# A chunk pair's triangular solve four pieces later in a slot pipeline, and DMA transfers in program order

## The chip, the core and the metric

The kernel runs on one core of one Trainium2 chip. The metric is the device time of one execution in microseconds. Engines are named as in the profile: PE (TensorE matrix multiplication), DVE (VectorE), ACT (ScalarE), POOL (GpSimd), SP (SyncE, whose queue issues every DMA transfer of this kernel). Tiles in PSUM are the banks that PE writes.

## What is computed

A linear recurrence with a decayed state over 768 steps (batch 4, 8 heads, head dimension 40), then a dense layer pair, then eight experts whose outputs are summed under weights that are normalised over tokens and experts.

```
for t in range(S):                                     # S = 768
    kt, vt, rt = (k[:, :, t], v[:, :, t], r[:, :, t])
    wt, at, bt = (w[:, :, t], a[:, :, t], b[:, :, t])
    y[:, :, t] = np.einsum('bhd,bhde->bhe', rt, state)
    Sa = np.einsum('bhde,bhe->bhd', state, at)
    state_decay = state * wt[:, :, None, :] - np.einsum('bhd,bhe->bhde', Sa, bt)
    state = state_decay + np.einsum('bhd,bhe->bhde', vt, kt)
...
h = x @ w_in                                           # 3072 x 320 by 320 x 2048
g = np.where(h > 0.0, h, alpha * (np.exp(np.minimum(h, 0.0)) - 1.0))
x = g @ w_out
...
for e in range(E):                                     # E = 8, 1024 wide
    h = np.maximum(x @ w1[e], 0.0)
    out += P[:, e:e + 1] * (h @ w2[e])
```

## The kernel before

The recurrence is cut into 24 chunks of 32 steps. Within a chunk the steps are made independent of each other by solving a unit lower triangular system of 32 x 32 for each of the 32 (batch, head) pairs. That solve is `tsolve_`: 31 columns, for each two DVE instructions, Tt = Wk x LT (L399) and Wk = Wk - Tt (L406). Wk starts as a copy of the identity, made by POOL (L394). LT, the matrix, is read from DRAM (L380), where E3 put it as Ad (four DMA transfers, L374) after PE (L355) and DVE (Am, L359) made it. The finished Wk goes to DRAM as Td in four transfers (L410) and comes back transposed as TT in four (L414). H2 (L447) multiplies by TT. Two chunks are solved together (`tsolve`), their instructions in turn.

The work of one chunk is a list of tokens, `PLAN["order"]`; one pass over it is a slot, and slot c finishes chunk c while it prepares chunks c+3 and c+4. E4 (L388) is the first matrix product of a slot. Then come, in this order: E3 for chunk c+3, H1, E2, H2, E1, H3, O1 (L500, transposes of VU into banks 2 and 3), H4, O2 (L355, whose result DVE masks as Gm, L359), O3a (L518, banks 2 and 3), O3b (L529). `prep` for chunk c+4 has its steps on DVE: wr and wq (L304, L305, from the loaded tile WA), the scan F (L308), the scan xE (L314). `xl` and `x` are the steps of the transposition of finished rows for the first dense layer, once in every two slots: two loads yt (L549), and for each half three transposes (L555, into bank 3), an ACT copy and X (L560, DVE, which reads bank 3). `ld`, `lu` and `lv` load WA and KE, VU, and rB and rO for coming chunks; yd (L537) stores the finished rows. `m` is half a unit of the first dense layer (L572 to L603), which fills PE between the steps of the recurrence; DVE makes g for it (L581).

There are 16 tokens `p` in a slot, counted here as p1 to p16. Each advances the pending solve by `PLAN["tp"]` = 3 steps. The token `T`, between p6 and p7 of an even slot c, puts the solve of chunks c+2 and c+3 in the queue; so it runs from p7 of the even slot to p11 of the odd one. The token `LT` is left out while a solve is pending.

From slot 2 on `pin_since` chains each instruction to the one before it on its engine, for the engines in `PINNED`: PE, DVE, ACT and POOL run in the order in which the code is written. SP isn't among them: a planner may put its transfers anywhere their data allow. Every transfer uses one of eight semaphores in turn, so that it waits for the landing of the transfer eight places ahead.

Behind slot 23 the rest of the first dense layer runs, and then the experts (`phase_b`), which take more than half of the time.

Of the kernel before, what the change touches and what calls it, by code (L numbers as in the profile page):

```python
# [22 lines left out]
PLAN = {  # L23
# [8 lines left out]
    "lead": 3,  # L32
}
# [64 lines left out]
def build(ctx, tc, r, k, v, w, a, b, w_in, w_out, wg, w1, w2, wa_d, kb_d, re_d, ro_d, vt_d, wp_d, consts, out, C, off):  # L98
# [11 lines left out]
    NB1 = NT // 256  # L110
    NTT = NT // 128
    V, A, G, T, SY = nc.vector, nc.scalar, nc.gpsimd, nc.tensor, nc.sync
    PINNED = {x.engine for x in (V, A, G, T)}
    pins = {}

    def traced():
        return nc.cur_bb.bb.instructions

    def pin_since(last):
        ins = traced()  # L120
        k = next(k for k in reversed(range(len(ins))) if ins[k] is last) + 1
        for x in ins[k:]:
            if x.engine in PINNED:
                if x.engine in pins:
                    tc.add_manual_dep(x, pins[x.engine], mybir.DependencyInfo(mybir.DependencyClass.NoSync, mybir.DependencyReason.DATA), reason="program order")
                pins[x.engine] = x.name
# [263 lines left out]
    def tsolve_(c):  # L390
        z = st[c]
        Wk = r2.tile([128, CI, C], F32, tag="Wk", name="Wk")
        tmp = r2.tile([128, CI * (C - 1)], F32, tag="Tt", name="Tt")
        G.tensor_copy(out=Wk.rearrange("p i t -> p (i t)"), in_=idk)  # L394
        for j in range(C - 1):
            ni = j // 4 + 1
            nt = C - 1 - j
            tv = tmp[:, 0:ni * nt].rearrange("p (i t) -> p i t", i=ni)
            V.tensor_tensor(  # L399
                out=tv,  # L400
                in0=Wk[:, 0:ni, j:j + 1].to_broadcast([128, ni, nt]),
                in1=z.LT[:, j, j + 1:C].unsqueeze(1).to_broadcast([128, ni, nt]),
                op=ALU.mult,
            )
            yield
            dve["T"] = V.tensor_tensor(out=Wk[:, 0:ni, j + 1:C], in0=Wk[:, 0:ni, j + 1:C], in1=tv, op=ALU.subtract)  # L406
            yield
        Td = drp.tile([B * H, C, C], F32, tag="Td", name="Td", bufs=3)
        for q in range(4):
            SY.dma_start(out=Td.rearrange("x (i q) t -> q x i t", q=4)[q], in_=Wk[q::4])  # L410
        z.TT = TTs[c % 4]
        for bb in range(B):
            bi = bb % 2
            SY.dma_start(out=z.TT[C * bb:C * bb + C, :, C * bi:C * bi + C], in_=Td[bb * H:(bb + 1) * H].rearrange("h s t -> s h t"))  # L414

    def tsolve(*cs):
        for _ in itertools.zip_longest(*(tsolve_(c) for c in cs)):
            yield
# [575 lines left out]
    with ExitStack():  # L994
# [13 lines left out]
        def try_xprep(new):  # L1008
            if new and not xgen:
                xp = ms["xp"]  # L1010
                if (late or xp == 0) and xp < NB1 and xp <= ms["n"] // NF1 + 1 and ("O3b", 2 * xp + 1) in done:
                    xgen.append(xprep(xp))
            if xgen and next(xgen[0], "end") == "end":
                xgen.pop()
                ms["xp"] += 1
# [41 lines left out]
        def advance(n, c):  # L1057
            if 0 <= c < NCH and (n, c) not in done:
                if (n, c) not in going:
                    going[(n, c)] = iter(fns[n](c) or ())  # L1060
                if next(going[(n, c)], "end") == "end":
                    done.add((n, c))

        pump = []

        def solve(n):
            for _ in range(n):
                if pump and next(pump[0], "end") == "end":
                    pump.pop(0)

        def conv(n):
            for _ in range(n):
                if wgen:
                    fn, *ar = wgen.pop(0)
                    cvd.add(("i" if fn is w_in_split else "o", ar[0]))
                    with tc.issue_after(dve["A"].ins) if "A" in dve else ExitStack():
                        fn(*ar)
                    if not wgen:
                        cvx.close()
                        late.append(moe.enter_context(tc.tile_pool(name="late", bufs=1)))  # L1080

        order = [(t.split("+")[0], int((t + "+0").split("+")[1])) for t in PLAN["order"].split()]
# [19 lines left out]
        for c in range(2, NCH + 1):  # L1102
            for n, o in order:
                last = traced()[-1]
                if n == "w":
                    conv(PLAN["wn"])
                elif n == "m":
                    acc += 3 if c < 5 else 4
                    if acc >= 4:
                        next(mg)  # L1110
                        acc -= 4
                elif n == "p":
                    solve(PLAN["tp"])
                elif n in ("x", "xl"):
                    try_xprep(n == "xl")
                elif n == "LT":
                    if not pump:
                        advance(n, c + o)
                elif n == "T":
                    if c % 2 == 0 and c + 3 < NCH:  # L1120
                        pump.append(tsolve(c + 2, c + 3))
                else:
                    advance(n, c + o)
                pin_since(last)
            st.pop(c - 2, None)
# [8 lines left out]
def _kern(tc, *aps, C=32, off=None):  # L1134
    with ExitStack() as ctx:
        build(ctx, tc, *aps, C=C, off=off)
# [30 lines left out]
```

## Time and profile before

| | us |
|---|---|
| median of three runs | 2373.11 (2370.55 to 2373.79) |
| profiled execution | 2378.4 |
| its span | 2376.6 |
| PE busy in the span | 2165.9 (91%) |
| DVE busy | 1017.4 (43%) |
| ACT busy | 742.1 (31%) |
| POOL busy | 490.0 (21%) |
| TensorE's granted clock, mean share | 0.975 |

Busy shares are means over stages with different limits: the slots of the recurrence lie between about 180 and 920 us, the experts behind 1010 us. So the windows by stage are read first, then the list of waits, then the timeline of single slots. A row of a timeline has the start, the length, engine, line, operation and tiles; in brackets the idle time of the engine before it and what ended it. The time that one engine names as a wait for another may go back to a DMA transfer for which that other one stood.

### The profile page before, as it was taken

What the parts mean: (1) busy time and instruction counts of PE and PEld (TensorE: products, weight loads), DVE (VectorE), ACT (ScalarE), POOL (GpSimd) and SP (SyncE); (2) the same over time, 40 slices, a digit from 0 to 9 for tenths busy, and PEclk for the clock granted to TensorE, in tenths of its full rate; (3) what the DMA queues carried; (4) which work ended last, traced back from release to release, by engine and by line L of the source; (5) the groups of instructions that cost most, each with busy time, mean ns of one, the idle gap of its engine ahead of it and who ended that gap; (6) DMA issues with size and microseconds to landing.
All of it is one profiled execution on the core that took longest, in us unless ns stands there. A gap on an engine that the chain in (4) does not pass through costs nothing.

```text
span 2376.6 us, 47915 instructions
## 1 busy us (share of the span) xinstructions
PE 2165.9 (91%) x19908; PEld 1976.0 (83%) x19908; DVE 1017.4 (43%) x2842; ACT 742.1 (31%) x1639; POOL 490.0 (21%) x608
## 2 busy tenths in 40 slices
PE   2348888998888999999999999999999999999998
PEld 2337788888787898989999999999999999999998
DVE  7978666667666652352222222222222222222222
ACT  2334444554444556422311211212212212112111
POOL 6333343333233325200200200101101002001000
PEclk9999999998889999999999999999999999999999
DMA  5342333332333313200100100100101001000000
GB/s 156 100 144 78 96 95 86 98 91 72 88 89 85 84 49 110 59 23 1 50 1 6 44 1 11 39 1 20 30 1 29 21 1 38 13 1 19 12 28 30
DMA packets 168458, 118.65 MB, mean 50 GB/s; under 512 B 102632, under 2 KB 148200, under 8 KB 168232
## 3 DMA queue, kind: packets, MB, share of 16 engines
q1 hardware_dynamic: 168232, 115.50, 17.7%
q8 instruction: 158, 2.59, 0.5%
q14 instruction: 68, 0.56, 0.1%
HBM read 96.97 MB, written 18.48 MB: 49 GB/s over the span
## 4 chain that ended last, share of the span: by engine, by line
PE 75%; DVE 11%; DMA 8%; SPq 2%; issue 2%; ACT 1%; POOL 1%; DVEq 0%; ACTq 0%; POOLq 0%
PE h L757 29%; PE pa L799 9%; PE pa L798 9%; PE pa L797 9%; PE ph L572 6%; DMA LT<-Ad 3%; DVE Wk L406 2%; PE a L599 2%; DVE Tt L399 2%; PE a L600 1%; PE a L601 1%; DMA Td<-Wk 1%; DVE F L308 1%; PE P L529 1%; PE P L355 1%
## 5 line engine op out<-in xcount | busy, mean ns | idle before, releaser
L757 PE MATMUL h<-X,a 128*128 128x512 f32 x3072 | 775.0, 394 | 0.0
L757 PEld LDWEIGHTS h<-X,a 128*128 128x128 f32 x3072 | 564.2, 188 | 102.9
L761 DVE SCALAR_TENSOR_TENSOR hl<-h,hh 128x512 fp32r<-128x512 f32 x384 | 264.9, 690 | 878.2 <-ACT hh L760 877.8
L760 ACT ACTIVATE hh<-h 128x512 fp32r<-128x512 f32 x384 | 230.3, 600 | 1021.8 <-PE h L757 1013.8
L798 PE MATMUL pa<-a,hl 128*128 128x320 f32 x1536 | 474.8, 310 | 0.0
L797 PE MATMUL pa<-a,hh 128*128 128x320 f32 x1536 | 472.2, 309 | 0.3 <-ACT logits L627 0.3
L799 PE MATMUL pa<-a,hh 128*128 128x320 f32 x1536 | 468.6, 309 | 0.0
L798 PEld LDWEIGHTS pa<-a,hl 128*128 128x128 f32 x1536 | 288.9, 188 | 15.9
L797 PEld LDWEIGHTS pa<-a,hh 128*128 128x128 f32 x1536 | 289.0, 188 | 14.8 <-ACT logits L627 0.4
L799 PEld LDWEIGHTS pa<-a,hh 128*128 128x128 f32 x1536 | 287.4, 188 | 0.0
L725 POOL TENSOR_TENSOR a<-rw,a 128x384 fp32r<-128x384 f32 x64 | 65.3, 1020 | 1055.7 <-ACT a L723 1050.2
L572 PE MATMUL ph<-X,Wt 128*128 128x256 f32 x1536 | 241.3, 303 | 0.6 <-DVE g L581 0.6
L585 POOL TENSOR_TENSOR gl<-g,gh 128x256 fp32r<-128x256 f32 x192 | 143.5, 750 | 420.3 <-ACT gh L583 337.6
L572 PEld LDWEIGHTS ph<-X,Wt 128*128 128x128 f32 x1536 | 210.8, 204 | 4.5 <-DVE g L581 0.8
L399 DVE TENSOR_TENSOR Tt<-Wk,LT 128x28 f32<-128x28 f32 (+24 forms) x744 | 165.7, 257 | 61.2 <-DMA LT<-Ad 38.0
L406 DVE TENSOR_TENSOR Wk<-Wk,Tt 128x28 f32<-128x28 f32 (+24 forms) x744 | 178.4, 275 | 2.2
L581 DVE SCALAR_TENSOR_TENSOR g<-m,ph 128x256 f32<-128x256 f32 x192 | 80.3, 418 | 211.6 <-ACT m L575 172.4
L583 ACT ACTIVATE gh<-g 128x256 fp32r<-128x256 f32 x192 | 80.1, 417 | 185.8 <-DVE g L581 183.7
L808 DVE SCALAR_TENSOR_TENSOR acc<-pa,Pg,acc 128x320 f32<-128x320 f32 x168 | 84.3, 544 | 114.8 <-PE pa L799 114.8
L574 ACT ACTIVATE m<-ph 128x256 f32<-128x256 f32 x192 | 73.5, 383 | 149.0 <-PE ph L572 143.8
L575 ACT ACTIVATE m<-m 128x256 f32<-128x256 f32 x192 | 80.0, 417 | 5.8
L599 PE MATMUL a<-gh,WoB 128*128 128x256 f32 x216 | 73.7, 341 | 1.3 <-ACT gh L583 1.3
(169 smaller groups left out, 2331.4 us busy)
## 6 DMA issues: line engine op xcount, KB each, us to landing
LT<-Ad SPq DMA_DIRECT2D x24, 512.0 KB
rw<-in_moe_w SPq DMA_DIRECT2D x64, 160.0 KB
WA<-in_wa SPq DMA_DIRECT2D x24, 416.0 KB
KE<-in_kb SPq DMA_DIRECT2D x24, 416.0 KB
rw<-in_moe_w SPq DMA_DIRECT2D x64, 128.0 KB
VU<-in_vt SPq DMA_DIRECT2D x24, 320.0 KB
raw<-in_wp SPq DMA_DIRECT2D x16, 384.0 KB
raw<-in_moe_w_out SPq DMA_DIRECT2D x16, 320.0 KB
```

The lines of the kernel that those rows point to most:

```text
L399: V.tensor_tensor(out=tv, in0=Wk[:, 0:ni, j:j + 1].to_broadcast([128, ni, nt]), in1=z.LT[:, j, j + 1:C].unsqueeze(1).to_broadcast([128, ni ...
L406: dve["T"] = V.tensor_tensor(out=Wk[:, 0:ni, j + 1:C], in0=Wk[:, 0:ni, j + 1:C], in1=tv, op=ALU.subtract)
L572: T.matmul(ph, lhsT=Wt[0:kp, wi, 128 * f:128 * f + 128], rhs=X[0:kp, xi, :], start=(i == 0), stop=(i == 7))
L585: G.tensor_tensor(out=gl, in0=g, in1=gh.bitcast(F32), op=ALU.subtract)
L599: T.matmul(o, lhsT=Wo(f)[:, 128 * i:128 * i + 128], rhs=gh, start=(s and i == 0), stop=False, skip_group_check=True)
L757: T.matmul(h, lhsT=a1[:, wi, :], rhs=X[bk][:, xi, :], start=(i == 0), stop=(i == 7))
L760: A.activation(out=hh, in_=h, func=AF.Relu)
L761: V.scalar_tensor_tensor(out=hl, in0=h, scalar=0.0, in1=hh.bitcast(F32), op0=ALU.max, op1=ALU.subtract)
L797: T.matmul(o, lhsT=hh[:, ts_], rhs=a2[:, 0, :], start=(f == 0), stop=False)
L798: T.matmul(o, lhsT=hl[:, ts_], rhs=a2[:, 0, :], start=False, stop=False)
L799: T.matmul(o, lhsT=hh[:, ts_], rhs=a2[:, 1, :], start=False, stop=(f == NF2 - 1))
L808: V.scalar_tensor_tensor(out=at, in0=o, scalar=Pg[:, tt, e:e + 1], in1=at, op0=ALU.mult, op1=ALU.add)
```

## The change

Four edits. A `yield` behind the copy of the identity makes the copy a step of its own, and the token `T` takes that one step at once. The other steps are taken only after a new token `G`, which stands behind the second half of O2 and the second step of `prep`, between p10 and p11. `tp` becomes 3 steps a piece in even slots and 4 in odd ones. And SP is added to `PINNED`.

```
-    "order": "... O1 p H4 m YW+1 prep+4 p O2 m O2 prep+4 p x m prep+4 x p O3a m p O3b ... LT+3 w",
+    "order": "... O1 p H4 m YW+1 prep+4 p O2 m O2 prep+4 G p x m prep+4 x p O3a m p O3b ... LT+3 w",
...
-    "tp": 3,
+    "tp": (3, 4),
...
-    PINNED = {x.engine for x in (V, A, G, T)}
+    PINNED = {x.engine for x in (V, A, G, T, SY)}
...
         G.tensor_copy(out=Wk.rearrange("p i t -> p (i t)"), in_=idk)
+        yield
         for j in range(C - 1):
...
-        pump = []
+        pump, pumping = [], []
 
         def solve(n):
             for _ in range(n):
                 if pump and next(pump[0], "end") == "end":
                     pump.pop(0)
+                    pumping.pop()
...
                 elif n == "p":
-                    solve(PLAN["tp"])
+                    if pumping:
+                        solve(PLAN["tp"][c % 2])
+                elif n == "G":
+                    if pump and not pumping:
+                        pumping.append(True)
...
                 elif n == "T":
                     if c % 2 == 0 and c + 3 < NCH:
                         pump.append(tsolve(c + 2, c + 3))
+                        next(pump[0])
```

Three places show what moved. Line numbers of the changed code are larger by up to seven. The first is SP's queue from the end of a solve in an odd slot into the following even slot. Before:

```order
L410 DMA Td<-Wk 256x1x32 x6
L414 DMA TT_109<-Td 32x8x32 x4
L410 DMA Td<-Wk 256x1x32 x2
L537 DMA yd<-xT 128x384
L296 DMA rO<-in_ro 104x512
L414 DMA TT_110<-Td 32x8x32 x4
L549 DMA yt<-yd 128x384
L374 DMA Ad<-Am_118 32x8x32 x4
L282 DMA WA<-in_wa 104x1024
L380 DMA LT<-Ad 128x1x1024
L284 DMA KE<-in_kb 104x1024
```

With the change:

```order
L411 DMA Td<-Wk 256x1x32 x4
L415 DMA TT_109<-Td 32x8x32 x4
L411 DMA Td<-Wk 256x1x32 x4
L415 DMA TT_110<-Td 32x8x32 x4
L538 DMA yd<-xT 128x384
L380 DMA LT<-Ad 128x1x1024
L294 DMA rB<-in_re 40x8x64 x2
L296 DMA rO<-in_ro 104x512
L550 DMA yt<-yd 128x384 x2
L374 DMA Ad<-Am_118 32x8x32 x4
L380 DMA LT<-Ad 128x1x1024
L289 DMA VU<-in_vt 128x640
```

Behind the last row follow WA and KE. The first LT, rB and the first yt stood further up before, the first LT just ahead of the first Td; WA stood ahead of the second LT and now stands behind it.

The second place is DVE in an even slot, from the X of the first half to the scan F. Before:

```order
L399 TENSOR_TENSOR Tt<-Wk,LT 128x31 x2
L406 TENSOR_TENSOR Wk<-Wk,Tt 128x31 x2
L399 TENSOR_TENSOR Tt<-Wk,LT 128x30 x2
L560 TENSOR_TENSOR X<-P_102,X 128x3x128
L478 TENSOR_TENSOR Y<-P_99,Yw 104x8x40
L478 TENSOR_TENSOR Y<-P_100,Yw 104x8x40
```

With the change:

```order
L561 TENSOR_TENSOR X<-P_102,X 128x3x128
L479 TENSOR_TENSOR Y<-P_99,Yw 104x8x40
L479 TENSOR_TENSOR Y<-P_100,Yw 104x8x40
L582 SCALAR_TENSOR_TENSOR g<-m,ph 128x256
L424 COPY uE<-P_102 80x512
L304 TENSOR_SCALAR wr<-WA 104x16x32
L305 TENSOR_SCALAR wq<-WA 104x16x31
L582 SCALAR_TENSOR_TENSOR g<-m,ph 128x256
L359 TENSOR_TENSOR Gm<-P_101,cst 64x16x32 x2
L308 SCALAR_TENSOR_TENSOR F<-wr,dr 104x528
L400 TENSOR_TENSOR Tt<-Wk,LT 128x31 x2
```

The first step of the solve, which reads LT, stood ahead of X and now stands behind F.

The third place is DVE in an odd slot, around wr and Gm. Before:

```order
L399 TENSOR_TENSOR Tt<-Wk,LT 128x24 x2
L304 TENSOR_SCALAR wr<-WA 104x16x32
L305 TENSOR_SCALAR wq<-WA 104x16x31
L406 TENSOR_TENSOR Wk<-Wk,Tt 128x8x3 x2
L399 TENSOR_TENSOR Tt<-Wk,LT 128x16 x2
L406 TENSOR_TENSOR Wk<-Wk,Tt 128x8x2 x2
L581 SCALAR_TENSOR_TENSOR g<-m,ph 128x256
L359 TENSOR_TENSOR Gm<-P_101,cst 64x16x32 x2
```

With the change:

```order
L304 TENSOR_SCALAR wr<-WA 104x16x32
L305 TENSOR_SCALAR wq<-WA 104x16x31
L400 TENSOR_TENSOR Tt<-Wk,LT 128x28 x2
L407 TENSOR_TENSOR Wk<-Wk,Tt 128x7x4 x2
L400 TENSOR_TENSOR Tt<-Wk,LT 128x24 x2
L407 TENSOR_TENSOR Wk<-Wk,Tt 128x8x3 x2
L582 SCALAR_TENSOR_TENSOR g<-m,ph 128x256
L359 TENSOR_TENSOR Gm<-P_101,cst 64x16x32 x2
```

Between wq and Gm four steps of the solve stand (a step is one row here, one instruction for each chunk) where three stood.

## Rows read from the trace of the kernel before

**Rows 1.** window: us, busy us (count) of PE PEld DVE ACT POOL, clock, DMA share, GB/s
```profile
240.00:841.00 601.00, 526.77 (x8765) 493.31 (x8765) 390.83 (x1431) 286.15 (x725) 219.03 (x279) 0.92 0.34 87
```

**Rows 2.** waits of the whole span: total us, times, longest us
```profile
DVE Tt L399 <- DMA LT<-Ad: 38.0, 10, 6.3
...
PE P L500 <- DVE X L560: 37.3, 9, 5.9
...
PE P L518 <- DVE X L560: 24.6, 9, 3.5
```

**Rows 3.** timeline of PE, slot 12 (even): start us, us, group [idle before <-releaser]
```profile
518.79 1.13 PE L388 MATMUL P<-VU,Am 128*64 128x40 f32 x32
...
531.54 0.55 PE L555 MATMUL P<-cst,yt 128*128 128x128 f32 x3 [1.10 <-ACT KB L423]
...
550.70 0.76 PE L518 MATMUL P<-Ss,rO 40*32 40x40 f32 x32 [2.93 <-DVE X L560]
```

**Rows 4.** timeline of PE, slots 4 and 18 (even) and 11 (odd)
```profile
240.19 1.13 PE L388 MATMUL P<-VU,Am 128*64 128x40 f32 x32
...
272.85 0.49 PE L518 MATMUL P<-Ss,rO 40*32 40x40 f32 x32 [3.48 <-DVE X L560]
...
512.82 0.78 PE L518 MATMUL P<-Ss,rO 40*32 40x40 f32 x64 [0.59 <-ACT m L574]
...
735.29 1.13 PE L388 MATMUL P<-VU,Am 128*64 128x40 f32 x32
...
768.88 0.76 PE L518 MATMUL P<-Ss,rO 40*32 40x40 f32 x32 [2.77 <-DVE X L560]
```

**Rows 5.** timeline of DVE, slot 12
```profile
537.62 0.19 DVE L399 TENSOR_TENSOR Tt<-Wk,LT 128x31 f32<-128x31 f32 x1 [2.89 <-DMA LT<-Ad]
...
542.43 0.42 DVE L304 TENSOR_SCALAR wr<-WA 104x512 f32<-104x512 f32 x1
...
545.24 1.38 DVE L359 TENSOR_TENSOR Gm<-P,cst 64x512 f32<-64x512 f32 x2
...
548.83 1.23 DVE L314 TENSOR_TENSOR_SCAN xE<-wq,dq 104x512 f32<-104x512 f32 x1
...
550.09 0.56 DVE L560 TENSOR_TENSOR X<-P,X 128x384 fp32r<-128x384 f32 x1
```

**Rows 6.** chain of waits, its DMA pieces: start us, us, what
```profile
192.70 2.02 DMA Td<-Wk
...
523.51 3.72 DMA yd<-xT
...
529.24 1.66 DMA Ad<-Am
...
531.05 6.48 DMA LT<-Ad
...
588.49 3.79 DMA Td<-Wk
```

**Rows 7.** timeline of SP's queue, slots 11 to 14
```profile
510.15 1.63 SPq L294 DMA_DIRECT2D rB<-in_re  x2
...
514.72 4.07 SPq L410 DMA_DIRECT2D Td<-Wk  x6
...
523.51 0.55 SPq L537 DMA_DIRECT2D yd<-xT  x1
...
527.77 1.93 SPq L374 DMA_DIRECT2D Ad<-Am  x4
...
592.35 1.80 SPq L414 DMA_DIRECT2D TT<-Td  x4
```

**Rows 8.** windows, columns as in rows 1: three transfers in slot 12; slot 11; slot 12
```profile
529.80:537.60 7.80, 4.96 (x93) 4.31 (x91) 0.77 (x2) 4.42 (x12) 2.13 (x4) 1.00 0.66 184
...
488.90:518.80 29.90, 29.31 (x523) 27.67 (x522) 22.15 (x89) 16.65 (x43) 9.81 (x13) 1.00 0.34 91
...
518.80:560.50 41.70, 34.54 (x517) 32.28 (x516) 24.50 (x82) 17.36 (x44) 16.34 (x22) 0.84 0.33 85
```

2 rows, old and new, of the table PLAN are left out of this document.

## Prediction

> **What bounds the kernel now.** I read four views in this order. The windows by stage show where TensorE is not yet the limit: between 240 and 841 us PE is busy 527 of 601 us at a mean granted clock of 0.92 [rows 1]. Behind the slots the change has nothing, so everything is decided there, in slots 4 to 22. The list of waits names what PE lacks: 37.3 us in nine waits at L500 and 24.6 us in nine at L518, both put down to DVE's L560 (X), and DVE itself waits 38.0 us in ten for the DMA of LT [rows 2]. The timeline of slot 12 joins them. DVE reaches the first step of a solve and sits until 537.62 for LT [rows 5]; X, which frees PSUM bank 3, is queued behind it on DVE, and PE stands at L500. Later in the slot PE stands 2.93 us at L518 until the second X (550.09 to 550.65) [rows 3, 5]. An even slot thus takes 41.7 us at a mean clock of 0.84, an odd one without these stalls 29.9 us at 1.00 [rows 8]. The reader is to see in the chain of waits why LT is late: SP issues Td, TT, yd, yt, Ad one after the other, LT follows Ad's landing at 531.05 and lands 6.48 us later [rows 6]. With the first Td issue at 514.72 [rows 7] as origin, which I call S (it follows the end of a solve at once), LT leaves at S+16.3 and lands at S+22.8. The next even slot's E4 (L388) starts at 518.79 [rows 3], S+4.1.
>
> A useful measure is the time from the E4 of an even slot to the restart of L518 after X: 32.7 us in slot 4, 33.6 in slot 18 [rows 4], 31.9 in slot 12 [rows 3]; over the eight even slots 4 to 18 the mean is 32.7. What follows to the next E4 is 9.8 us in slot 12 (41.7 less 31.9 [rows 3, 8]); the same work in odd slot 11 takes 6.0 (512.82 to 518.79 [rows 3, 4]), since there the clock is not halved.
>
> **The change, part by part.**
>
> *G and the copy ahead.* The steps of the solve leave p7 to p10 of the even slot and the two copies of Wk stay where they were on POOL. The first LT read now stands on DVE behind wr, wq, Gm and F. LT's lateness hits nobody there as long as LT has landed when F is done. In front of PE's L500 DVE then holds only X and Y, so the waits at L500 (37.3 us in nine [rows 2], about 4 each) go. The two copies cost nothing: POOL had that work at that place already.
>
> *Four steps a piece in odd slots.* The solve must still end in p11 of the odd slot. DVE does 12 steps more in that slot than before. It is busy 22.2 of 29.9 us there [rows 8], and a step on both chunks is two instructions of about 0.2 us (the first L399 [rows 5]), so 4 to 5 us fit into 7.7 us idle. They do not fit everywhere: from the middle of the slot DVE has little idle time, and the pieces p7 to p10 put Gm about 0.6 us later and p11 brings S to 0.9 us later. PE's L518 in an odd slot stands directly behind Gm (0.59 us of wait already [rows 4]), so I charge 0.6 us to every odd slot. The bounds are 0, if the idle time takes it, and 1.5, if none does.
>
> *SP in program order.* This is the part that decides. Before, the planner put six Td, four TT, two Td in a row; the wait for one Td set lay under the issue of the other, one yt was loaded a slot ahead, and WA left ahead of LT. Now SP runs, from S on: four Td, their landing, four TT, four Td, their landing, four TT, yd, LT, rB twice, rO, yt twice, four Ad, their landing, LT, VU, WA, KE. A Td issue is 0.68 (4.07 over 6 [rows 7]) and its landing 2.02 from its issue with nothing ahead [rows 6]: a set of four takes 3 x 0.68 + 2.02 = 4.05. Four TT take 1.80 [rows 7], with the gap 1.85. So 11.8 for both chunks. yd 0.6 [rows 7], LT the same: 13.0. rB 1.65 [rows 7]: 14.7; rO, as one more issue, 0.4: 15.1, where the first yt leaves; two yt 1.2: 16.3; Ad three quarters of 1.93 [rows 7], then 1.66 to landing [rows 6]: 19.4. The second LT thus leaves at S+19.4 instead of S+16.3, and VU and WA follow behind it. Each wait of SP here holds the whole rest of the list: that is the price of program order.
>
> WA is what DVE needs next: wr (L304) reads it, and wr now is where the LT wait was. LT, VU and WA are 512, 320 and 416 KB, 1.28 MB. While WA, LT and KE were in flight the queue moved 184 GB/s over 7.8 us [rows 8], so 6.9 us: WA lands at S+26.3. The low end is LT's own 6.48 [rows 6]; the high end is LT's 6.48 and then VU and WA at that rate, 4.0 more, 10.5 us. The two Td landings have 3.79 as their high end [rows 6], when something large is ahead of them. I take 2.02, since after this order nothing is.
>
> From wr to the end of X DVE took 542.43 to 550.65, 8.2 us, in slot 12 [rows 5]; the three solve steps that stood between wq and Gm are gone, 0.9 us: 7.3. X then ends at S+26.3+7.3 = S+33.6. With S 0.9 later and the odd slot 0.6 longer, E4 is at S+3.8, so L518 restarts at E4+29.8. Before it was 32.7 on the mean. An even slot gains 2.9, an odd one loses 0.6: 2.3 for a pair, 18 us for the eight pairs.
>
> *yt.* It leaves at S+15.1 and lands 2.0 to 3.7 us later (the landings of Td and yd [rows 6]). PE's L555 is due at 531.54 less its 1.10 of wait [rows 3], S+15.7. So PE will wait there 1.5 to 3 us in every even slot. In slots 4 to 18 this lies under the wait for WA that comes later in the slot and costs nothing more; if WA were early it would be the next thing late. In slot 20 it replaces the LT wait. In slot 22, which had no solve and no wait, it costs 2.4 and some clock, 4 us. ACT's copy of xT, which waits for yd, comes about a microsecond later too and lies under the same wait.
>
> The sum: -18 + 4 = -14 us. The profiled execution took 2378.4 us with a span of 2376.6; the median of the three runs, 2373.1, is 0.2% below it. I put the difference to the median: 2359.
>
> The Trainium skill speaks against my main term: "DMA: Bandwidth & Descriptors", section "Issuing engines are not separate DMA queues", holds the time a sequencer takes to initiate a DMA for usually small beside the DMA itself. By it SP's order would cost almost nothing and the sum would be that of the first rival. Here the trace disagrees: six Td issues hold SP for 4.07 us, twice the 2.02 us of one landing [rows 6, 7].
>
> **The rivals.**
>
> *The order on SP is cheap and WA is on time.* Then the L500 waits go without a successor: 32.7 less about 4.1 (37.3 over 9 [rows 2]), less 0.9 for the three steps, less a microsecond of halved clock, is E4+26.7. That is 6.0 - 0.6 = 5.4 for a pair, 43 us for eight, with 2 to 5 more in slot 20: 2326. For it: DMA is busy only a third of the stage [rows 1]. Against it: the issue times above are measured, and 19.4 us of them stand between S and the second LT.
>
> *The gain is eaten by the clock.* PE's wait at L518 grows, since it arrives there earlier while X is set by WA. After such a wait the clock was halved in slot 12, and the rest of the slot took 9.8. The nine even slots of the window average 40.2 us (601 less eight odd slots of 29.9, over nine [rows 1, 8]), so some of them had a shorter tail, about 8.3. If now all eight take 9.8, 1.5 x 8 = 12 us are lost again: 2371, no change.
>
> *SP's list becomes the loop, and it is slower.* If Td lands in 3.8 instead of 2.0 (1.8 each, 3.5 for both) and WA takes 8 us instead of 6.9, X ends 4.6 us later, at E4+34.4. Then an even slot loses 1.7 and an odd one 0.6: 18 us for eight pairs, and 4 for slot 22: 2395. It decides from 2.3 us later than my sum, E4+32.1. For it: three other chains of the trace show Td landings above 3 us, one of them at 588.49 [rows 6]. Against it: in the trace LT leaves just ahead of Td there, and in the new order it does not.
>
> **How the numbers follow.** A difference under 0.2% (5 us) is about what a measurement of this kernel cannot tell from none. My forecast, 2359, has 0.47; the cheap order, 2326, 0.15; the clock, 2371, 0.18; the slower loop, 2395, 0.20. Faster is the first two, 0.62; same 0.18; slower 0.20. For the range, half of the slower loop and half of the cheap order are left out: 2328 to 2390, which takes in 2 us either way for a pair (eight pairs, 16 us) around the forecast.
>
> **What would show it.** In the profile after: DVE's wait for LT falls from 38 us to under 10, and the waits at L500 nearly vanish; DVE waits for WA at L304, 1 to 4 us in each of eight even slots; PE waits at L518 grow from 24.6 to over 30; PE waits 1 to 3 us at L555 in even slots (put down to yt or to ACT's KB); the second LT leaves SP at S+18 to S+21; L518 in even slots restarts at E4+29 to E4+31; odd slots take 30 to 31 us. If L304 does not wait and even slots take under 37 us, the cheap order is right; if L518 restarts later than E4+32, the slower loop is; if it restarts at 30 and even slots still take 41, the clock. The prediction is wrong altogether if slots 4 to 20 keep their length for another reason, such as TT landing too late for H2 (L447), which the sum puts 4 us ahead of need.

## The result and the profile after

The changed kernel takes 2406.55 us (2403.07 to 2406.72) against 2371.95 for the kernel before on the same chip: a ratio of 1.0142, 95% interval 1.0124 to 1.0159. It is 1.4% slower, and 17 us above the top of the forecast range. The profiled execution has a span of 2404.7 us, 28.1 more than before.

The window that answers to [rows 1] says that the loss is idle time and clock, not work (columns as there):

```profile
240.00:841.00 601.00, 524.96 (x8473) 492.70 (x8471) 372.78 (x1367) 275.61 (x705) 214.24 (x271) 0.89 0.32 86
```

In the same 601 us PE did 8473 matmuls instead of 8765, at a mean granted clock of 0.89 instead of 0.92.

The list of waits of the changed kernel answers to [rows 2] (total us, times, longest us; L500 is L501 now, L518 is L519, L555 is L556, L560 is L561):

```profile
ACT xT L424 <- DMA yd<-xT: 32.8, 7, 6.1
DVE wr L304 <- DMA WA<-in_wa: 31.8, 13, 6.4
...
PE P L519 <- DVE X L561: 25.4, 9, 3.4
PE P L556 <- DMA yt<-yd: 25.2, 9, 4.7
...
PE P L337 <- ACT xT L424: 13.2, 5, 4.2
...
DVE Tt L400 <- DMA LT<-Ad: 1.7, 1, 1.7
```

DVE's wait for LT fell from 38.0 to 1.7 us, and the 37.3 us that PE stood at L501 for X are gone. So the first two edits do what they were forecast to do. In their place stand three waits for other transfers: yd, yt and WA. All three come out of one list, SP's queue. It is shown here from the end of the solve in slot 11 (531.79, the S of the prediction) into slot 12, and answers to [rows 7] (start us, time that the issues took, line, tiles, count):

```profile
531.79 2.55 SPq L411 DMA_DIRECT2D Td<-Wk  x4
535.84 1.81 SPq L415 DMA_DIRECT2D TT<-Td  x4
537.70 2.48 SPq L411 DMA_DIRECT2D Td<-Wk  x4
542.68 1.79 SPq L415 DMA_DIRECT2D TT<-Td  x4
544.52 0.45 SPq L538 DMA_DIRECT2D yd<-xT  x1
545.01 1.26 SPq L380 DMA_DIRECT2D LT<-Ad  x1
546.31 1.71 SPq L294 DMA_DIRECT2D rB<-in_re  x2
548.13 0.46 SPq L296 DMA_DIRECT2D rO<-in_ro  x1
548.64 0.82 SPq L550 DMA_DIRECT2D yt<-yd  x2
549.56 1.86 SPq L374 DMA_DIRECT2D Ad<-Am  x4
553.59 0.61 SPq L380 DMA_DIRECT2D LT<-Ad  x1
554.24 0.59 SPq L289 DMA_DIRECT2D VU<-in_vt  x1
554.92 2.21 SPq L282 DMA_DIRECT2D WA<-in_wa  x1
557.24 0.32 SPq L284 DMA_DIRECT2D KE<-in_kb  x1
```

The yd leaves 12.73 us after S, 8.63 of them issue time of the sixteen Td and TT and the rest two landings; before, it left 8.79 after S (523.51 less 514.72, [rows 7]). Over the even slots 4 to 18 yd leaves at S+12.7 to S+14.3. The first yt leaves at S+16.85, before at S+12.55. PE meets this list in slot 12, which answers to [rows 3]:

```profile
538.78 1.13 PE L388 MATMUL P<-VU,Am 128*64 128x40 f32 x32
...
552.20 0.52 PE L556 MATMUL P<-cst,yt 128*128 128x128 f32 x3 [1.83 <-DMA yt<-yd]
...
565.40 0.51 PE L519 MATMUL P<-Ss,rO 40*32 40x40 f32 x32 [2.33 <-ACT m L575]
569.30 0.76 PE L519 MATMUL P<-Ss,rO 40*32 40x40 f32 x32 [3.38 <-DVE X L561]
```

DVE meets it later in the same slot, at wr:

```profile
562.92 0.43 DVE L304 TENSOR_SCALAR wr<-WA 104x512 f32<-104x512 f32 x1 [4.88 <-DMA WA<-in_wa]
```

The chain of waits of the changed kernel (start us, us, what) puts the two transfers in this slot on the path that ends last, as [rows 6] did with LT. In slot 14 the path is SP's list from the end of a solve on (the row at 606.48 is the landing of the first set of Td):

```profile
548.64 3.42 DMA yt<-yd
552.20 0.52 PE P L556 x3
...
554.92 7.97 DMA WA<-in_wa
...
606.48 3.23 DMA Td<-Wk
...
613.51 3.39 DMA Td<-Wk
...
629.26 7.81 DMA WA<-in_wa
```

Over the even slots 4 to 18 WA stands on this chain in seven of eight, yt in three. wr waits for WA in all eight, 0.3 to 4.9 us.

Windows of slot 11, slot 12, the tail of slot 11 and the time from the issue of WA to its landing (columns as in [rows 1]; the first two answer to [rows 8]):

```profile
505.09:538.78 33.69, 32.24 (x521) 30.55 (x520) 26.64 (x112) 17.11 (x44) 12.71 (x16) 0.90 0.28 70
538.78:577.84 39.06, 31.52 (x515) 29.49 (x515) 17.74 (x53) 15.95 (x41) 12.99 (x18) 0.87 0.36 99
...
529.90:538.70 8.80, 8.80 (x128) 8.45 (x128) 4.63 (x15) 2.76 (x6) 5.57 (x6) 0.61 0.20 32
...
554.90:562.90 8.00, 8.00 (x92) 7.77 (x91) 1.56 (x4) 3.28 (x8) 2.11 (x3) 1.00 0.73 211
```

Slot 11 grew from 29.90 to 33.69 us, and most of what it lost lies in a tail of 8.80 us at a clock of 0.61.

Over slots 4 to 19 of the two profiled executions, in means worked out from the starts of E4 (L388): an even slot takes 41.27 us instead of 40.99, an odd one 32.04 instead of 29.88. So a pair loses 2.45, and eight pairs 19.6. Slot 22 loses 8.7 more, slot 21 0.9, slot 20 gains 2.1, and what lies ahead of slot 4 loses 2.1. Together that is 29.3 us; the spans differ by 28.1.

### The profile page after: what moved, and what is told of

Read it like the earlier page. It is cut to its first block, busy times and chain, and to the rows that moved or that the text cites. A ratio compares the mean times of both kernels' runs of the same rounds, so it can differ in the third digit from the quotient of the medians.

```text
span 2404.7 us, 47882 instructions
## 1 busy us (share of the span) xinstructions
PE 2180.0 (91%) x19908; PEld 1991.3 (83%) x19908; DVE 1019.2 (42%) x2842; ACT 739.8 (31%) x1639; POOL 491.7 (20%) x608
## 3 DMA queue, kind: packets, MB, share of 16 engines
q1 hardware_dynamic: 168232, 115.50, 17.3%
## 4 chain that ended last, share of the span: by engine, by line
PE 74%; DVE 10%; DMA 8%; SPq 3%; issue 2%; POOL 2%; ACT 1%; DVEq 0%; ACTq 0%; POOLq 0%
PE h L758 30%; PE pa L799 9%; PE pa L800 9%; PE pa L798 9%; PE ph L573 5%; DMA WA<-in_wa 3%; DVE Wk L407 2%; DVE Tt L400 2%; PE a L600 2%; DMA Td<-Wk 1%; PE a L601 1%; PE a L602 1%; PE P L530 1%; DVE F L308 1%; SPq L415 1%
## 5 line engine op out<-in xcount | busy, mean ns | idle before, releaser
L400 DVE TENSOR_TENSOR Tt<-Wk,LT 128x28 f32<-128x28 f32 (+24 forms) x744 | 157.7, 248 | 3.6 <-DMA LT<-Ad 1.7
L337 PE MATMUL P<-cst,KE 104*128 104x104 f32 x192 | 30.0, 308 | 54.0 <-POOL KE L324 24.7
```

The costliest lines, as they stand in the source:

```text
L400: V.tensor_tensor(out=tv, in0=Wk[:, 0:ni, j:j + 1].to_broadcast([128, ni, nt]), in1=z.LT[:, j, j + 1:C].unsqueeze(1).to_broadcast([128, ni ...
```

## The experiments

Three explanations stood against each other. **The list**: an even slot now runs on SP's list; from the end of a solve SP must work off Td, TT, Td, TT, yd and yt in order before PE can go on at L556, and what an odd slot gains, the next even slot gives back. **WA**: of the late transfers only WA matters. **The pieces**: the loss sits in DVE's longer pieces of the solve in the odd slots and in the halved clock behind them, and SP's lateness only follows. The quoted expectations call them by letters. A is that SP's order is the cause, in the first ones through WA above all, in the later ones through the list. C, and B from the trial with both Td first on, is the pieces; where a letter stands for something else, the expectation says so.

Ratios are to the kernel before on the same chip, whose median was 2371.95 to 2379.39 us from chip to chip, so ratios are compared and not times. The means per slot are worked out from E4's starts in slots 4 to 19 of the profiled execution, with L556 counted from E4 of its even slot and L519 from there to its restart behind X.

| kernel | median us | ratio (95%) | even | odd | L556 | L519 |
|---|---|---|---|---|---|---|
| before | 2371.95 | 1 | 40.99 | 29.88 | 12.1 | 32.7 |
| changed | 2406.55 | 1.0142 (1.0124 to 1.0159) | 41.27 | 32.04 | 16.3 | 33.1 |
| changed, SP free | 2338.66 | 0.9861 (0.9821 to 0.9901) | 34.07 | 32.02 | 12.1 | 26.2 |
| again | 2339.84 | 0.9826 (0.9799 to 0.9854) | 34.71 | 32.21 | 12.4 | 26.5 |
| before, SP pinned | 2425.53 | 1.0209 (1.0161 to 1.0256) | 44.77 | 29.84 | 17.3 | 35.7 |
| WA earlier | 2406.04 | 1.0134 (1.0086 to 1.0183) | 40.09 | 32.31 | 16.0 | 32.0 |
| p10 behind Gm | 2407.91 | 1.0156 (1.0105 to 1.0206) | 43.38 | 29.88 | 18.2 | 35.1 |
| Td of both first | 2386.75 | 1.0036 (1.0021 to 1.0052) | 38.83 | 31.89 | 14.2 | 30.4 |
| yt earlier | 2402.40 | 1.0087 (1.0068 to 1.0106) | 40.20 | 31.86 | 14.5 | 31.8 |
| yt and WA earlier | 2379.25 | 1.0007 (0.9988 to 1.0025) | 38.88 | 31.11 | 15.5 | 30.7 |
| all four by hand | 2349.20 | 0.9855 (0.9818 to 0.9892) | 37.03 | 30.33 | 14.6 | 29.5 |
| SP free, p10 behind Gm | 2330.27 | 0.9787 (0.9770 to 0.9803) | 35.68 | 29.88 | 13.4 | 27.4 |
| again | 2332.12 | 0.9789 (0.9763 to 0.9815) | 35.78 | 29.87 | 13.3 | 27.4 |

**The change without the order on SP.**

```
-    PINNED = {x.engine for x in (V, A, G, T, SY)}
+    PINNED = {x.engine for x in (V, A, G, T)}
```

> The changed kernel without SP in program order: the solve behind G, the copy ahead and the four-step pieces stay. Theory A (SP's program order ate the gain: WA lands 31 us after the solve's end and holds wr, X and L519 up): WA leaves ahead of LT again, LT's wait is hidden by G, even slots 4 to 18 restart L519 some 27 us behind E4 instead of 33 and take 34 to 37 us; odd slots keep the 32 us of the changed kernel, since the pieces of four stay; slot 22 is back at 26. Time about 2340 (2325 to 2360). Theory B (placing the solve behind G brings nothing by itself; what was lost are the odd slots, 17 us, and slot 22): about 2380 to 2390.

It is 1.4% faster than before. L519 restarts at E4+26.2: the solve moved down is worth the six microseconds in an even slot that the first rival of the prediction names. The window and one of the waits:

```profile
240.00:841.00 601.00, 556.79 (x9489) 523.94 (x9485) 405.05 (x1525) 307.74 (x785) 235.58 (x295) 0.95 0.36 90
...
DVE wr L304 <- DMA WA<-in_wa: 9.0, 4, 5.3
```

No wait of PE for the DMA of yt is left. The odd slots are as long as in the changed kernel (32.02), so that part of the loss has nothing to do with SP.

**The order on SP alone**, in the kernel before.

```
-    PINNED = {x.engine for x in (V, A, G, T)}
+    PINNED = {x.engine for x in (V, A, G, T, SY)}
```

> The kernel before with SP in program order and nothing else changed: the solve still begins at T with pieces of three. Theory A: the second LT leaves 21 to 22 us behind the solve's end instead of 16.3 and WA behind it, and at T nothing hides LT: DVE waits about 5 us longer for LT in each even slot, slot 22 loses 8 us: 2410 to 2430. Odd slots stay at 29.9. Theory B (SP's order is nearly free, since the transfers are hidden): 2370 to 2380.

It costs 2.1% by itself, with the odd slots unchanged at 29.84 and the even ones 3.8 us longer. The waits for yd, yt and LT in this kernel:

```profile
ACT xT L423 <- DMA yd<-xT: 45.8, 9, 6.4
PE P L555 <- DMA yt<-yd: 30.5, 9, 5.9
...
DVE Tt L399 <- DMA LT<-Ad: 27.7, 10, 6.0
```

The time is what A expected, the place is not: DVE's wait for LT was to grow by some 5 us in each even slot, and it fell from 38.0 to 27.7 us in all. The waits that grew are those for yd and yt.

So the order on SP turns a gain of 1.4 to 1.7% into a loss of 1.4%. The Trainium skill ("DMA: Bandwidth & Descriptors", section "Issuing engines are not separate DMA queues") holds initiating time for usually small beside the DMA itself; for this list the trace disagrees: in slot 12 of the changed kernel 8.63 us of issues stand in front of yd, beside 3.42 us from the issue of yt to its landing.

**WA ahead of Ad and LT**, with SP in program order (loads of WA become a step of their own):

```
-    "order": "lv E4 m prep+3 p E3+3 xl m E3+3 p H1 ...
+    "order": "lv E4 m prep+3 p E3+3 xl lw+4 m E3+3 p H1 ...
```

> The changed kernel, SP in program order, with the load of WA for chunk c+4 moved ahead of Ad and LT in the list of tokens (KE stays where it was). Theory A: WA leaves about 17 us behind the solve's end and lands by 23, before wr is due; DVE's wait for WA goes, LT lands later but is hidden behind G; L519 in even slots restarts at E4+28 to 30 instead of 33: 8 x 4 = 30 us less, 2370 to 2382. If the even slots are bound by something else (L556's wait for yt, the scans and X, or the clock) the time stays at 2400 to 2407.

A miss. WA came in time and nothing was won: in the profiled execution the even slots 4 to 18 are 1.2 us shorter, slots 20 and 22 are 4.7 and 1.9 us longer. The waits:

```profile
ACT xT L429 <- DMA yd<-xT: 35.4, 9, 6.1
PE P L561 <- DMA yt<-yd: 26.8, 9, 6.2
...
DVE wr L309 <- DMA WA<-in_wa: 8.9, 4, 5.3
```

The wait for WA is back to the four of the kernel without order on SP, and wr waits for it in none of the even slots 4 to 18, yet PE still stands for yt (L561 here). The chain of waits now goes through yt in all eight of these slots; in slot 12 it reads:

```profile
540.98 1.99 DMA yd<-xT
...
544.39 4.27 DMA yt<-yd
```

L519 restarts at S+37.4 on the mean, against S+37.9 in the changed kernel. So WA alone isn't the cause: it is one of several late transfers in a row, and behind it stands another that holds PE nearly as long.

**The piece p10 behind Gm**, with SP in program order.

```
-    ... YW+1 prep+4 p O2 m O2 prep+4 G p x ...
+    ... YW+1 prep+4 O2 m O2 p prep+4 G p x ...
```

> The changed kernel with the piece of the solve p10 moved behind the mask Gm, in the list of tokens, and nothing else. Theory C (the odd slots lost 2.1 us each because four steps instead of three stand between wq and Gm: PE's wait at L519 went from 0.59 to 1.45 us, and in four of the eight odd slots the granted clock fell behind it): the wait goes under 0.6 us, odd slots return to 29.9 to 30.5, 12 to 17 us less: 2390 to 2395. If the odd slots are longer for another reason (the pieces p1 to p9, or later KE), they stay at 32 and the time at 2403 to 2407.

The odd slots return to 29.88, all eight of them, so the pieces in front of Gm were what lengthened them. But the total does not move: the even slots take back 2.1 of the 2.2 us. Slots 11 and 12 show how (rows of PE, then of SP):

```profile
525.20 0.78 PE L519 MATMUL P<-Ss,rO 40*32 40x40 f32 x64 [0.59 <-ACT m L575]
531.18 1.13 PE L388 MATMUL P<-VU,Am 128*64 128x40 f32 x32
549.11 0.87 PE L556 MATMUL P<-cst,yt 128*128 128x128 f32 x3 [3.73 <-DMA yt<-yd]
```

```profile
527.99 2.55 SPq L411 DMA_DIRECT2D Td<-Wk  x4
```

From the end of the solve to L556 it is 21.1 us (549.11 less 527.99); in the changed kernel it is 20.4 in this slot and 20.4 to 22.0 in all eight. PE comes to E4 earlier and waits longer. That is the loop, and it speaks against the pieces as the cause of the total: a shorter odd slot is worth nothing while this list stands. The changed kernel shows the same by itself: from slot 7 to slot 18 an odd slot and the even one behind it take 72.0 to 73.8 us together, whether the odd one took 30.7 or 33.7.

**Both chunks' Td ahead of the first TT.** Within the solve's generator:

```
             SY.dma_start(out=Td...[q], in_=Wk[q::4])
+        if pump:
+            yield
         z.TT = TTs[c % 4]
```

> The changed kernel with one thing altered: both chunks' Td transfers leave ahead of the first TT, so SP no longer stands for the landing of the first Td and the landing of the second lies partly under the first TT. Theory A (the loop is SP's list from the end of a solve over Td, TT, yd to the landing of yt): SP's yd leaves about 3.2 us earlier after the end of a solve (12.7 us before), the eight even slots lose 3 us each, 25 us together: 2375 to 2388. Theory B (the loss sits in DVE's pieces in the odd slots and in the halved clock behind them; SP's lateness only follows from it): no change, 2400 to 2410.

The list holds. One landing and a part of the other vanish from the list, seen here in slots 11 and 12:

```profile
520.45 5.17 SPq L411 DMA_DIRECT2D Td<-Wk  x8
525.78 4.93 SPq L417 DMA_DIRECT2D TT<-Td  x8
530.82 0.39 SPq L540 DMA_DIRECT2D yd<-xT  x1
```

The yd leaves at S+10.4 instead of S+12.7 in these slots, an even slot takes 2.4 us less, and the ratio falls from 1.0142 to 1.0036. The work on PE, DVE and ACT in these slots is unchanged, as is its order: only what SP stood for has gone.

**The two yt ahead of rB and rO.**

```
-    "order": "lv E4 m prep+3 p E3+3 xl m E3+3 ...
+    "order": "xl lv E4 m prep+3 p E3+3 m E3+3 ...
```

> The changed kernel with the two loads of yt ahead of rB and rO on SP, nothing else moved. yt then leaves about 2 us earlier (1.8 us for two rB, 0.5 for rO, less what SP now waits for the landing of yd). Theory A: PE reaches L556 that much earlier, 1 to 2 us for each of nine even slots: 2388 to 2400. Theory B: no change, 2400 to 2410.

L556 comes 1.8 us earlier after E4, but the even slots shrink by only 1.1, since DVE now waits 48.0 us in thirteen for WA instead of 31.8: most of what PE gains at L556 comes back as a longer wait for WA. The median of 2402.40 lies 2.4 above the list's expectation and within that of the pieces; but the kernel before took 2379.39 beside it, and the ratio fell by 0.55%, 13 us, which is what the list expected. Taken alone this run would not decide.

**Both yt and WA earlier.**

```
-    "order": "lv E4 m prep+3 p E3+3 xl m E3+3 ...
+    "order": "xl lv E4 m prep+3 p E3+3 lw+4 m E3+3 ...
```

> The changed kernel with both moves at once that brought little alone: yt ahead of rB and rO, and WA ahead of Ad and LT. Theory A (yt and WA stand one behind the other in an even slot: with yt early PE still waits for X behind WA, with WA early PE still waits for yt, so each move alone shows little): together they give what yt brings, 1.8 us in each of nine even slots, and PE's wait at L519 falls with it: ratio to the kernel before 0.998 to 1.006. Rival (the gains add, and neither is hidden by the other): about the product of the two alone, 1.0134 and 1.0087 against 1.0142: 1.008.

Alone the two moves brought 0.1 and 0.55%, together 1.35%: either late transfer had hidden most of what moving the other is worth. The ratio lies where the list put it and below the 1.008 of two moves that merely add. What is late next can be read off slot 12 of this kernel (ACT, then PE; L429 is the copy of xT, L561 the transposes of yt):

```profile
529.46 0.43 ACT L429 COPY xT<-P 128x320 f32<-128x320 f32 x1 [4.56 <-DMA yd<-xT]
```

```profile
529.94 0.93 PE L342 MATMUL P<-cst,KE 104*128 104x104 f32 x8 [1.49 <-ACT xT L429]
533.67 0.55 PE L561 MATMUL P<-cst,yt 128*128 128x128 f32 x3 [1.83 <-ACT KB L429]
```

The copy of xT needs the buffer that yd is still storing, PE stands for the copy, and the transposes stand behind KB, which ACT copies after it. So behind yt comes yd, and it hangs on the same list.

**All four moves by hand**: both Td first, yt earlier, WA earlier, and p10 behind Gm, with SP still in program order.

```
-    "order": "lv E4 m prep+3 p E3+3 xl m E3+3 ... prep+4 p O2 m O2 prep+4 G p x ...
+    "order": "xl lv E4 m prep+3 p E3+3 lw+4 m E3+3 ... prep+4 O2 m O2 p prep+4 G p x ...
...
+        if pump:
+            yield
         z.TT = TTs[c % 4]
```

> The changed kernel with SP still in program order, but with four moves in that order: both Td sets ahead of the first TT, yt ahead of rB and rO, WA ahead of Ad and LT, and the piece p10 behind Gm. Theory A: SP's list up to yt is 5 us shorter after the end of a solve and WA, which none of these waits now hides, lands in time; the odd slots give 2 us each: 7 to 8 us a pair, 2335 to 2350. Theory B: only the odd slots' 2 us a pair come back, 2385 to 2395.

At 0.9855 nearly all that SP's order had cost is back, with SP still in program order. So it is mostly this order that was slow and not the fixing of one. With p10 at the same place and SP free the ratio is 0.9787 (below), so the planner's order is still 0.7% better than this one; there yd leaves at S+8 to S+9, here at S+10 to S+11.

**SP free, and p10 behind Gm**, twice, the second time beside the same kernel without that move.

```
-    ... YW+1 prep+4 p O2 m O2 prep+4 G p x ...
+    ... YW+1 prep+4 O2 m O2 p prep+4 G p x ...
...
-    PINNED = {x.engine for x in (V, A, G, T, SY)}
+    PINNED = {x.engine for x in (V, A, G, T)}
```

> The changed kernel without program order on SP, and with the piece p10 moved behind the second step of O2, so that DVE makes Gm ahead of it. Theory A: with SP's list out of the loop nothing gives the odd slots' gain back; odd slots return from 30.7 to 34.0 us to 29.9, the even ones stay at 31 to 36: 16 to 20 us less than the 2338.7 without this move, 2318 to 2325. Rival (the even slots give it back, as they did with SP in program order): 2334 to 2342.

> The changed kernel without program order on SP, again, beside the next kernel on the same chip: ratio 0.982 to 0.990, as the first time.

> The same with p10 behind Gm, again. If the odd slots' gain stays, as theory A has it: 0.7 to 0.9% below the kernel of the run above. If the even slots give it back: within 0.3% of it.

This is the best kernel, 2.1% below the one before in both runs. Side by side it is 0.4% below the same kernel without the move (0.9789 against 0.9826, with intervals that overlap a little), so neither expectation was right: the odd slots gain 2.3 us and the even ones give 1.1 of it back. ACT's waits for yd rise from 3.3 us in two to 9.7 in seven, which fits the same loop (from slot 6 on E4 comes at S+2.75 there, at S+3.6 or later without the move). That yd is the cause was not tried and stays open.

## Why the prediction was wrong

*The part that held.* G and the copy ahead: the waits at L501 go, LT is no longer waited for, the copies cost nothing. The kernel with SP free puts the worth of this at 1.4 to 1.7%. From wr to the restart of L519 7.3 us were forecast, and 6.9 is the mean. The first rival's restart of E4+26.7 is what that kernel shows (26.2).

*The step that failed* is the sum of "SP in program order" and, behind it, the step called "yt". Two places wait for SP's list, and both were put too early.

The first is wr, which waits for WA; the forecast was built from it. WA lands at S+31.1 on the mean of the eight even slots, not at S+26.3, and so L519 restarts at S+37.9, not at S+33.6. The path was the right one and its length was 4.8 us short.

The second is PE at L556. The prediction says that its wait there "lies under the wait for WA that comes later in the slot and costs nothing more". With WA as late as it was, the wait did lie there: with yt earlier, most of the gain at L556 came back as a longer wait for WA. But a wait is covered only as long as the later one lasts, and PE comes to L556 later than was forecast: at S+21.2 on the mean, not at S+17.2 to S+18.7. Its wait there, 1.1 to 3.8 us, is about what was forecast. What was put at about a microsecond, and at nothing in the sum, is xT: yd leaves late, ACT waits for it, and in five of the eight slots PE stands 1.6 to 4.2 us for ACT's copy at L337, ahead of L556. The trial with WA earlier shows the worth of this path: WA was in time, and L519 restarted at S+37.4. So with WA in time little of the forecast gain comes; both have to be earlier, as the trial with both moves shows. The loop had to be closed, too: yt and yd hang on S, S on the odd slot, the odd slot on the even slot's end.

*The terms of the list*, from S on:

| step | forecast | slot 12 | even slots 4 to 18 |
|---|---|---|---|
| first Td set with landing | 4.05 | 4.05 | 3.95 to 5.25 |
| second Td set with landing | 4.05 | 4.98 | 3.9 to 5.7 |
| first LT issue | 0.6 | 1.26 | 0.56 in the other seven |
| first yt leaves | S+15.1 | S+16.85 | S+16.5 to S+17.7 |
| yt lands after | 2.0 to 3.7 | 3.42 | 3.4 to 4.3 in the three on the chain |
| second LT leaves | S+19.4 | S+21.8 | S+21.8 to S+23.4 |
| second LT to the landing of WA | 6.9 | 9.30 | 7.9 to 9.3 |

In slot 22 PE's wait for yt, forecast at 2.4 us, was 4.74.

The 2.02 us for a landing held for the first Td in five of the eight slots, and for the second in two of the six that stand on the chain: the choice "since after this order nothing is" ahead of it took the low end without a row for a second set. For WA three transfers, 1.28 MB, were counted. The window shows that more was moved: 211 GB/s over 8.0 us are 1.69 MB, that is LT, VU, WA and also KE (416 KB), which left behind WA. At the prediction's own rate, 184 GB/s, the four take 9.2 us. That KE delays WA is read off these bytes and was not tried by itself.

*Odd slots.* 0.6 us was charged, the bound was 1.5, and 2.2 were lost. The direct part is 0.86 (PE's wait before L519 went from 0.59 to 1.45 in every odd slot), inside the bounds. The rest is the clock: after that wait four of the eight odd slots ran their tail at the lower level and took 32.3 to 33.7 us, the others 30.7. The prediction applied the halved clock to even slots alone. With p10 behind Gm wait and loss both vanish, but the even slots take back what the odd ones gain: the lost 2.2 us are not a part of the total that stands by itself.

*Which rival came.* "SP's list becomes the loop, and it is slower": L519 restarts at E4+33.1, beyond its point of decision, E4+32.1. Its 3.8 us for a Td landing were above the second set's (2.0 to 3.4 us in the six that stand on the chain), its 8 us for WA near the 7.9 to 9.3. Its loss of 2.3 us for a pair is nearly the 2.45 measured, though it had most of it in the even slot; its 2395 is short mainly of slots 21 and 22, which lose 9.6 us instead of 4, and the medians differ by 34.6 us where the profiled spans differ by 28.1. It had a chance of 0.20. What spoke for it stood in the prediction's own words, "each wait of SP here holds the whole rest of the list"; the argument against it was a transfer order, not a row.

## What to carry to other kernels

When an engine whose queue holds nothing but transfers is put in program order, write out its list from the event that starts it to each transfer that someone waits for, and close the loop: what waits for the last of them, and how that reaches the starting event again. A wait that precedes a longer one is covered only while the longer one lasts, so size both: where two late transfers of one list hide each other, mending both brings more than the two trials alone add up to. If moving one late transfer ahead brings nothing, move two at once before you drop the theory.

## What the runs showed of the hardware

The same wait did not always bring the same clock. In slots 11 and 13 of the changed kernel PE waited 1.45 us before L519, both times after a stretch at full clock. These rows are the wait in slot 11, the wait in slot 13, and the window behind the second (the one behind the first stands above, at 0.61):

```profile
529.85 0.78 PE L519 MATMUL P<-Ss,rO 40*32 40x40 f32 x64 [1.45 <-ACT m L576]
```

```profile
602.60 0.78 PE L519 MATMUL P<-Ss,rO 40*32 40x40 f32 x64 [1.45 <-ACT m L576]
```

```profile
603.00:608.50 5.50, 5.50 (x107) 5.21 (x92) 4.28 (x15) 1.96 (x5) 2.62 (x4) 1.00 0.19 31
```

Slot 11 took 33.7 us and slot 13 30.7. In the two kernels in which only p10 was moved behind Gm, with SP free and with SP in program order, the wait is 0.59 us and every odd slot takes 29.9 us. What decides at 1.45 us stays open.
